# A windowed attention and a gated feed-forward in one kernel: the inverse of the fourth head pair becomes a list item of its own

## The chip, the cores and the metric

The kernel runs on one core of one Trainium2 chip. The metric is the device time of one execution in microseconds. Below, TensorE is PE in the profile's rows (its weight loads are PEld), VectorE is DVE, ScalarE is ACT, GpSimd is POOL and SyncE is SP. All five run their own instruction streams and wait for each other by semaphores.

## The reference

Attention for 4 batches, 8 heads, 768 positions and 64 channels per head, with a mask that keeps the first 8 keys and the last 96 keys before each query, and a bias that falls with distance. Its output, 3072 tokens of 512 channels, goes straight into a feed-forward with a ReLU gate:

```
scores = scale * q @ k.T + bias(head, distance);  masked where neither global nor local
a = exp(scores - max);  a = a / (sum(a) + 1e-9)
x = (a @ v), heads side by side                      # 3072 x 512
out = (relu(x @ w_gate) * (x @ w_val)) @ w_out       # 512 -> 1536 -> 512
```

## The kernel before

**Halves.** The work is cut into eight halves of 384 tokens (a batch has two). For each half c there is attention, which fills the tile xT (the attention output, transposed, 128 x 4 x 384), and the feed-forward, which reads it. Attention of half c+1 is woven into the feed-forward of half c: the halves 2 to 7 are made by `attention_pieces(s)`, and the weaving runs in the feed-forward of half 1 (with the rest of half 0) and of halves 2 to 6. These are the "later halves" of the change. Halves 0 and 1 are written out by hand with other functions, and the feed-forward of half 7 has no attention beside it.

**Feed-forward of a half.** Twelve blocks f = 0 to 11 of hidden channels. For each block a gate product g(f), four matmuls with 384 columns into one PSUM bank (L745), which ACT empties with a ReLU into the tile grelu (L754), and a value product v(f), four more matmuls, which DVE multiplies with the ReLU into ht (L761). Then the output products, seven groups p1, p2, p4, p6, p5, p7, p3 for a pair of token tiles (L631; a Strassen-like scheme whose sums of ht, the tiles hsum, DVE makes at L624 to L627, whose first result ACT copies at L660, and whose other results DVE adds at L644). Odd halves from 3 on have seven more, for a pair of tiles across two halves. So an even half has 24 + 7 = 31 products and an odd half 24 + 14 = 38; the first weave, in halves 0 and 1, has 38 too.

**Attention of a half.** Four pairs of heads p = 0 to 3. The list that `attention_pieces` returns has these items: U0, U1, U2 score two groups each (L512, four PSUM banks, of which the first is from the pool of two "av" banks and three are from the pool of three "qk" banks); X takes one of those banks through the exponential on ACT (L521) and puts the mask multiplication of the one before it on DVE (L533); AVp, two items e = 0 and 1 for the two heads, multiplies the weights with the values (L431, one "av" bank each; half of the 128 rows is the sum of the weights, which the ones beside the values give) and puts the logarithm of that sum on ACT (L440, tile lnd). The second of the two also puts the exponential of minus the logarithm, the inverse, on ACT (L445, tile rcp). Np, the norms, are two DVE multiplications of 64 rows by 384 columns (L450), which write xT, read the "av" banks and so set them free.

**Order.** The kernel writes its own order; every engine takes its instructions in the order in which the code gives them. `weave` walks through the products of the feed-forward, all of equal weight, and after each of them puts out the attention items whose place has been reached. The places come from `spread`, which divides a stretch evenly by the number of items in the list:

```
n = len(items)
return [(first + (i + 0.5) / n * (last - first), f) for i, (_, f) in enumerate(items)]
```

The stretch is 0.02 to 0.86 of the products in the first weave, 0 to 0.87 in even halves and 0 to 0.85 in odd ones. "Place k" below is the place straight after the k-th product of the weave: in even and odd halves g(0) is product 1, v(0) product 2, up to v(11), product 24, and p1 is product 25. The list also holds empty items (`wait`) that only take a share of the stretch.

**Banks.** PSUM has eight banks here: three of the pool "qk", two of "av", three of "ff" (the products of the feed-forward). When a tile is asked for, the pool gives the bank that was set free first, and the first matmul into it waits for whoever read that bank last.

Of the kernel before, what the change touches and what calls it, by code (L numbers as in the profile page):

```python
# [8 lines left out]
FP32 = mybir.dt.float32  # L9
BF16 = mybir.dt.bfloat16  # L10
FP16 = mybir.dt.float16
AF = mybir.ActivationFunctionType
# [4 lines left out]
def kernel(  # L17
# [12 lines left out]
    nc = tc.nc  # L30
# [6 lines left out]
    N_DC = DM // 128  # L37
    N_FC = DFF // 128
    HP = H // 2
    QH = S // 2  # L40
# [6 lines left out]
    scale = 1.0 / math.sqrt(D)  # L47
# [22 lines left out]
    rc_pool = ctx.enter_context(tc.tile_pool(name="rc", bufs=2))  # L70
    xt_pool = ctx.enter_context(tc.tile_pool(name="xt", bufs=3))
# [180 lines left out]
    xT_of = {}  # L252
    es_of = {}
    av_of = {}
# [165 lines left out]
    def piece_av(s, p, e):  # L420
        b, half = divmod(s, 2)
        h = 2 * p + e
        vb = vbuf[b % 2]
        av = av_psum.tile([128, 512], FP32, name="av_ps")
        av_of[s, p, e] = av
        av3 = av[:, 0:QH].rearrange("d (n p) -> d n p", n=NN)
        todo = [t for bank in banks_of_half[half] for t in bank]
        for i, (j, a, w, m) in enumerate(todo):
            es, c = es_of[s, p, j, e]
            z0 = 2 * D * h + (D if e == 0 else 0)  # L430
            nc.tensor.matmul(av3[:, :, a : a + w],  # L431
                             lhsT=vb[:, j, z0 : z0 + 128],
                             rhs=es[:, c : c + NN * w].rearrange("k (n p) -> k n p", n=NN),
                             start=(i == 0), stop=(i == len(todo) - 1),
                             skip_group_check=True)
        o0, d0 = (0, 64) if e == 0 else (64, 0)
        if e == 0:
            av_of[s, p, "l"] = rc_pool.tile([128, QH], FP32, name="lnd")
        ln = av_of[s, p, "l"]
        nc.scalar.activation(ln[o0 : o0 + 64], av[d0 : d0 + 64, 0:QH], AF.Ln, bias=0.0, scale=1.0)  # L440
        if e == 1:
            if s not in xT_of:
                xT_of[s] = xt_pool.tile([128, N_DC, QH], BF16, name="xT")
            rc = rc_pool.tile([128, QH], FP32, name="rcp")
            nc.scalar.activation(rc, ln, AF.Exp, bias=0.0, scale=-1.0)  # L445
            av_of[s, p, "r"] = rc

    def piece_norm(s, p, e):
        r = slice(64 * e, 64 * e + 64)
        nc.vector.tensor_tensor(xT_of[s][r, p, :], av_of[s, p, e][r, 0:QH], av_of[s, p, "r"][r],  # L450
                                op=ALU.mult)

    def piece_av_wide(s, p, *pools):

        b, half = divmod(s, 2)
        todo = [t for bank in banks_of_half[half] for t in bank]
        pools = pools or (AVB,)
        av = [pool.tile([128, 512], FP32, name=name) for pool, name in (pools[0], pools[-1])]
        for what in range(2):
            av3 = av[what][:, 0:QH].rearrange("d (n p) -> d n p", n=NN)  # L460
            for i, (j, a, w, m) in enumerate(todo):
                for e in range(2):
                    es, ce = es_of[s, p, j, e]
                    z0 = D + 2 * D * (2 * p + e)
                    nc.tensor.matmul(av3[64 * e : 64 * e + 64, :, a : a + w],  # L465
                                     lhsT=ones if what == 0 else vbuf[b % 2][:, j, z0 : z0 + D],
                                     rhs=es[:, ce : ce + NN * w].rearrange("k (n p) -> k n p", n=NN),
                                     start=(i == 0), stop=(i == len(todo) - 1),
                                     skip_group_check=True)
        av_of[s, p] = av  # L470

    def piece_norm_wide(s, p):
        piece_sums_wide(s, p)
        piece_mul_wide(s, p)
# [20 lines left out]
    def score_unit(s, groups, pools):  # L495


        b, half = divmod(s, 2)
        out = []
        for pp, g in groups:  # L500
            banks = []
            for e in range(2):
                pool, name = pools.pop(0)
                banks.append(pool.tile([128, 512], FP32, name=name))
                out.append((pp, g, e, banks[e]))
            c = 0
            for j, a, w, m in banks_of_half[half][g]:
                for p in (2 * pp, 2 * pp + 1):
                    for e in range(2):
                        r = slice(64 * e, 64 * e + 64)  # L510
                        q3 = qT2[s % 2][r, p].rearrange("d (n p) -> d n p", n=NN)
                        nc.tensor.matmul(banks[e][:, c : c + NN * w], lhsT=kT[b % 2][p][r, j, :],  # L512
                                         rhs=q3[:, :, a : a + w], start=True, stop=True)
                    c += NN * w
        return out

    def unit_exp(s, pp, g, e, ps):
        bank = banks_of_half[s % 2][g]
        cols = sum(2 * NN * w for _, _, w, _ in bank)
        es = es_pool.tile([128, 480], BF16, name="es")  # L520
        nc.scalar.activation(es[:, 0:cols], ps[:, 0:cols], AF.Exp, bias=0.0, scale=scale)  # L521

        def mask():
            c = 0
            for j, a, w, m in bank:
                n_ = 2 * NN * w
                e4 = es[:, c : c + n_].rearrange("k (i n p) -> k i n p", i=2, n=NN)
                h0 = 4 * pp + e
                mk = m_all[:, h0 : h0 + 3 : 2, 0 if j == 0 else 1, :, m : m + w]
                if w == WQ:  # L530
                    e4 = e4.rearrange("k i n p -> k i (n p)")
                    mk = mk.rearrange("k i n p -> k i (n p)")
                nc.vector.tensor_mul(e4, e4, mk)  # L533
                for i in range(2):
                    es_of[s, 2 * pp + i, j, e] = (es, c + i * NN * w)
                c += n_

        return mask

    def attention_pieces(s):  # L540
        masks, units = [], []

        def flush():
            for f in masks:
                f()
            masks.clear()

        def scores(groups, pools):
            units.extend(score_unit(s, groups, list(pools)))

        def x(scored=None):
            ready = masks[:]
            masks.clear()
            if scored:
                scores(*scored)
            masks.append(unit_exp(s, *units.pop(0)))
            for f in ready:
                f()

        U = [([(0, 0), (0, 1)], (AVB, QKB, QKB, QKB)),  # L560
             ([(0, 2), (1, 0)], (AVB, QKB, QKB, QKB)),
             ([(1, 1), (1, 2)], (AVB, QKB, QKB, QKB))]
        X = lambda u=None: [(0.0, lambda: x(u))]
        AV = lambda p: [(0.0, lambda e=e: (flush(), piece_av(s, p, e))) for e in range(2)]
        N = lambda p: [(0.0, lambda: (piece_norm(s, p, 0), piece_norm(s, p, 1)))]
        wait = [(0.0, lambda: None)]
        a0, a1 = AV(0), AV(1)

        return (X(U[0]) + X() + X() + X() + wait + X(U[1]) + X() + X() + a0[0:1] + X() + a0[1:2] + N(0) + wait
                + X(U[2]) + X() + a1[0:1] + X() + X() + a1[1:2] + N(1) + wait * 2 + AV(2) + N(2) + wait * 2  # L570
                + AV(3) + N(3))


    out_v = out.rearrange("(s p n) d -> s n p d", p=128, n=NN)
# [262 lines left out]
    def AV(s, p, *pools):  # L837
        piece_av_wide(s, p, *pools)
        piece_norm_wide(s, p)
# [139 lines left out]
    def T2_piece(p):  # L979
# [10 lines left out]
    sums_wo = [(0.0, f) for i in (0, 3) for f in weight_sums(i, i + 3)]  # L990
    weave(f1_0[G[2]] + f1_1[G[2]] + f2_0 + f2_1,
          spread(attention_pieces(2), 0.02, 0.86), spread(early_pieces(3), 0.1, 0.76),
          spread(sums_wo, 0.08, 0.4))

    for c in range(2, NHALF):
        placed = []
        if c + 1 < NHALF:
            placed.append(spread(attention_pieces(c + 1), 0.0, 0.85 if c % 2 else 0.87))
        if c + 2 < NHALF:
            load_qk(c + 2, 0, H)  # L1000
            load_v_half(c + 2)
            placed.append(spread(early_pieces(c + 2), 0.25, 0.75))
        f1, f2 = ffn_pieces(c)
        weave(f1 + f2, *placed)
# [35 lines left out]
```

The softmax here doesn't subtract the row's maximum and nothing guards it: scores larger than these inputs give would overflow.

## Time and profile before

| What | Value |
|---|---|
| device time, median of 3 runs | 238.54 us (237.76 to 238.59) |
| profiled execution: span | 236.1 us |
| feed-forward of halves 2 to 7 starts at | 75.78, 100.33, 129.31, 154.04, 183.03, 207.58 us |
| so even halves 2, 4, 6 take | 24.55, 24.73, 24.55 us |
| and odd halves 3, 5 take | 28.98, 28.99 us |
| L440 logarithms | 48, 485 ns each |
| L445 exponentials of logarithms | 24, 523 ns each |
| L450 norms | 48, 553 ns each |
| L761 products of gate and value | 96, 557 ns each |
| L745 matmuls | 768, 155.8 us of PE's 228.7 us busy |

The starts of the halves are read from the timeline of PE, at the first gate product of each. In a timeline line the columns are the start (us), the length (us), the engine, the line of code, the operation with what it writes and reads, and how many instructions are merged; brackets hold idle time of the engine before it and what ended that. In a waits line the three numbers are the sum (us), how often, and the longest (us).

### The profile page before, as it was taken

The page shows a single profiled execution, that of the slowest core. Times are in us where ns is not written, and L with a number is a line of the kernel's source. Part 1 is how long each engine was busy: PE and PEld are TensorE (multiplying, and loading weights), DVE is VectorE, ACT ScalarE, POOL GpSimd, SP SyncE. Part 2 cuts the span into 40 slices and gives each one's busy share as a digit, 9 for nine tenths or more (in the row PEclk, how much of TensorE's full clock was granted, in tenths as well). Part 3 has the DMA queues.
Part 4 walks back from the last instruction along what each step waited for, and adds up shares of the span by engine and source line. Part 5 has one row for each costly group of instructions (what it writes and reads, how often), then busy time and mean ns, then how long its engine had stood idle before and what let it go on. Part 6 is the DMA issues. An engine that isn't in the chain of part 4 may idle for free.

```text
span 236.1 us, 5512 instructions
## 1 busy us (share of the span) xinstructions
PE 228.7 (97%) x2021; PEld 157.7 (67%) x2021; DVE 186.9 (79%) x466; ACT 146.2 (62%) x321; POOL 89.0 (38%) x191
## 2 busy tenths in 40 slices
PE   7898999999999999999999999999999999999994
PEld 3674766656678666856688566856688566865683
DVE  6876867879988779886999779876899779863784
ACT  7988865667624887467842787557742687624310
POOL 8997913933483066406580066405340000000000
PEclk9999999999999999999999999999999999999999
DMA  5999999998459856856397764846412200020005
GB/s 167 203 168 183 206 262 282 171 118 267 72 155 170 250 149 106 52 176 204 90 81 119 236 175 90 53 143 214 93 44 89 92 0 3 0 92 0 1 3 178
DMA packets 71419, 30.43 MB, mean 129 GB/s; under 512 B 47744, under 2 KB 70784, under 8 KB 71392
## 3 DMA queue, kind: packets, MB, share of 16 engines
q0 software_dynamic: 34896, 10.27, 38.7%
q1 hardware_dynamic: 36496, 19.82, 29.7%
q8 instruction: 16, 0.26, 0.5%
q14 instruction: 11, 0.09, 0.1%
HBM read 28.38 MB, written 6.29 MB: 147 GB/s over the span
## 4 chain that ended last, share of the span: by engine, by line
PE 83%; DVE 5%; POOL 4%; DMA 4%; ACT 2%; issue 1%; POOLq 0%; DVEq 0%
PE ff_ps L745 49%; PE ff_ps L631 19%; PE av_ps L431 6%; DMA kc<-in_q_dram 4%; PE ff_ps L778 2%; PE av_ps L512 2%; PE qk_ps L512 2%; POOL vbuf L154 1%; DVE wo_sum L597 1%; DVE obuf L644 1%; DVE ht L761 1%; DVE es L533 1%; POOL kc L131 1%; PE av_ps L465 1%; POOL wg L171 1%
## 5 line engine op out<-in xcount | busy, mean ns | idle before, releaser
L754 ACT ACTIVATE grelu<-ff_ps 128x384 bf16<-128x384 f32 x96 | 46.8, 489 | 52.6 <-PE ff_ps L745 39.3
L745 PE MATMUL ff_ps<-xT,wg 128*128 128x384 bf16 x384 | 77.9, 326 | 0.2 <-DMA wg<-in_moe_w_gate_dram 0.2
L745 PE MATMUL ff_ps<-xT,wv 128*128 128x384 bf16 x384 | 77.9, 326 | 0.0
L761 DVE TENSOR_TENSOR ht<-ff_ps,grelu 128x384 f16<-128x384 f32 x96 | 53.4, 557 | 27.6 <-PE ff_ps L745 23.5
L745 PEld LDWEIGHTS <-wv 128*128 128x128 bf16 x384 | 36.0, 98 | 23.9 <-issue 1.1
L745 PEld LDWEIGHTS <-wg 128*128 128x128 bf16 x384 | 36.3, 97 | 21.7 <-issue 0.7
L450 DVE TENSOR_TENSOR xT<-av_ps,rcp 64x384 bf16<-64x384 f32 x48 | 26.6, 553 | 6.1 <-ACT rcp L445 5.3
L367 POOL CAST kc<-ks 128x384 bf16<-128x384 f32 x20 | 10.6, 569 | 54.5 <-DMA ks<-in_k_dram 54.5
L644 DVE TENSOR_TENSOR obuf<-ff_ps,obuf 128x512 f32<-128x512 f32 (+1 forms) x46 | 27.6, 604 | 3.6 <-PE ff_ps L631 0.9
L440 ACT ACTIVATE lnd<-av_ps 64x384 f32<-64x384 f32 x48 | 23.3, 485 | 11.1 <-PE av_ps L431 10.2
L533 DVE TENSOR_TENSOR es<-es,m_all 128x432 bf16<-128x432 bf16 (+3 forms) x108 | 29.9, 321 | 0.2 <-ACT es L521 0.2
L521 ACT ACTIVATE es<-qk_ps 128x432 bf16<-128x432 f32 (+2 forms) x54 | 27.6, 531 | 0.0
L154 POOL DMA_DIRECT2D vbuf<-in_v_dram x29 | 24.7, 860 | 0.1
L431 PEld LDWEIGHTS <-vbuf 128*128 128x128 bf16 x216 | 18.2, 98 | 4.8 <-DVE xT L450 0.4
L431 PE MATMUL av_ps<-es,vbuf 128*128 128x216 bf16 (+4 forms) x216 | 21.4, 226 | 0.0
L631 PEld LDWEIGHTS <-ht 128*128 128x128 f16 x198 | 18.6, 97 | 3.5 <-issue 0.8
L631 PEld LDWEIGHTS <-hsum 128*128 128x128 f16 x192 | 18.5, 98 | 2.1
L631 PE MATMUL ff_ps<-wo_sb,ht 128*128 128x256 f16 x132 | 18.3, 272 | 0.0
L631 PE MATMUL ff_ps<-wo_sum,hsum 128*128 128x256 f16 x144 | 17.2, 272 | 0.0
L445 ACT ACTIVATE rcp<-lnd 128x384 f32<-128x384 f32 x24 | 12.6, 523 | 0.8
L521 ACT ACTIVATE es<-av_ps 128x432 bf16<-128x432 f32 (+2 forms) x18 | 9.5, 527 | 2.0 <-PE qk_ps L512 2.0
L512 PEld LDWEIGHTS <-kT 64*128 64x128 bf16 x216 | 6.6, 94 | 6.1 <-issue 3.8
(130 smaller groups left out, 263.6 us busy)
## 6 DMA issues: line engine op xcount, KB each, us to landing
out_dram<-obuf SPq DMA_DIRECT2D x22, 256.0 KB
ks<-in_k_dram SPq DMA_DIRECT2D x5, 768.0 KB
qs<-in_q_dram SPq DMA_DIRECT2D x5, 768.0 KB
vbuf<-in_v_dram POOLq DMA_DIRECT2D x23, 120.0 KB, 4.7
wv<-in_moe_w_val_dram POOLq DMA_DIRECT2D x3, 512.0 KB, 10.5
wo_sb<-in_moe_w_out_dram POOLq DMA_DIRECT2D x1, 1536.0 KB, 21.0
wg<-in_moe_w_gate_dram POOLq DMA_DIRECT2D x2, 512.0 KB, 10.3
ks<-in_k_dram SPq DMA_DIRECT2D x4, 192.0 KB
```

The lines of the kernel that those rows point to most:

```text
L154: nc.gpsimd.dma_start(out=v_dst(b, NG + r0, NG + r0 + n, j), in_=v[b, :, KT * j + r0 : KT * j + r0 + n, :].rearrange("h p d -> p h d"))
L431: nc.tensor.matmul(av3[:, :, a : a + w], lhsT=vb[:, j, z0 : z0 + 128], rhs=es[:, c : c + NN * w].rearrange("k (n p) -> k n p", n=NN), star ...
L440: nc.scalar.activation(ln[o0 : o0 + 64], av[d0 : d0 + 64, 0:QH], AF.Ln, bias=0.0, scale=1.0)
L450: nc.vector.tensor_tensor(xT_of[s][r, p, :], av_of[s, p, e][r, 0:QH], av_of[s, p, "r"][r], op=ALU.mult)
L512: nc.tensor.matmul(banks[e][:, c : c + NN * w], lhsT=kT[b % 2][p][r, j, :], rhs=q3[:, :, a : a + w], start=True, stop=True)
L521: nc.scalar.activation(es[:, 0:cols], ps[:, 0:cols], AF.Exp, bias=0.0, scale=scale)
L533: nc.vector.tensor_mul(e4, e4, mk)
L631: nc.tensor.matmul(ps[:, c0 : c0 + DH], lhsT=lhs(i), rhs=rhs(i), start=(i == 0), stop=(i == NP - 1), skip_group_check=True)
L644: add = lambda o, x, y: nc.vector.tensor_tensor(o, x, y, op=ALU.add)
L745: nc.tensor.matmul(st[key][:, 0:QH], lhsT=w_of(w, dc, fc), rhs=xT_of[c][:, dc, :], start=(dc == 0), stop=(dc == N_DC - 1))
L754: nc.scalar.activation(gr, psg[:, 0:QH], AF.Relu, bias=0.0, scale=1.0)
L761: nc.vector.tensor_tensor(ht[:, fc, :], psv[:, 0:QH], st["r", fc], op=ALU.mult)
```

## The change

The exponential of the logarithms of pair 3 is taken out of the item that holds the second half of AV3 and becomes an item of the list by itself, between AV3 and its norms N3. It is meant to let other ACT work pass between logarithm and exponential, and to keep the norms from being queued on DVE before their factor is there. The pairs 0 to 2 keep logarithm and exponential in one item. The tile xT is asked for where the first norm is written, and no longer where the first exponential is; this moves no instruction.

```
-        if e == 1:
-            if s not in xT_of:
-                xT_of[s] = xt_pool.tile([128, N_DC, QH], BF16, name="xT")
-            rc = rc_pool.tile([128, QH], FP32, name="rcp")
-            nc.scalar.activation(rc, ln, AF.Exp, bias=0.0, scale=-1.0)
-            av_of[s, p, "r"] = rc
+        if e == 1 and p < HP - 1:
+            piece_inverse(s, p)
+
+    def piece_inverse(s, p):
+        rc = rc_pool.tile([128, QH], FP32, name="rcp")
+        nc.scalar.activation(rc, av_of[s, p, "l"], AF.Exp, bias=0.0, scale=-1.0)
+        av_of[s, p, "r"] = rc
 
     def piece_norm(s, p, e):
+        if s not in xT_of:
+            xT_of[s] = xt_pool.tile([128, N_DC, QH], BF16, name="xT")
...
         return (X(U[0]) + X() + X() + X() + wait + X(U[1]) + X() + X() + a0[0:1] + X() + a0[1:2] + N(0) + wait
                 + X(U[2]) + X() + a1[0:1] + X() + X() + a1[1:2] + N(1) + wait * 2 + AV(2) + N(2) + wait * 2
-                + AV(3) + N(3))
+                + AV(3) + [(0.0, lambda: piece_inverse(s, 3))] + N(3))
```

The list has 30 items before and 31 after.

## The prediction

> **What bounds the kernel now.** I read the page first: engine shares, the granted clock and the chain that ended last.
>
> ```profile
> PE 228.7 (97%) x2021; PEld 157.7 (67%) x2021; DVE 186.9 (79%) x466; ACT 146.2 (62%) x321; POOL 89.0 (38%) x191
> ...
> PEclk9999999999999999999999999999999999999999
> ...
> PE 83%; DVE 5%; POOL 4%; DMA 4%; ACT 2%; issue 1%; POOLq 0%; DVEq 0%
> ```
>
> TensorE is busy 97% of the span at full clock and carries 83% of the chain, so a wait put into its stream lengthens the kernel by its full length. The timeline says whether "busy" is also full speed: in an even half a product of four 384-column matmuls starts every 0.65 us (84.85 to 85.50 below), 162 ns a matmul, and the same from product to product. Waits that TensorE could still lose are few. The waits views of the weight loads and of VectorE, in that order, show where it is near to waiting:
>
> ```profile
> PEld L512 <- DVE xT L450: 2.1, 6, 0.5
> ...
> PEld L431 <- DVE xT L450: 0.4, 1, 0.4
> ```
>
> ```profile
> DVE xT L450 <- ACT rcp L445: 5.3, 14, 0.9
> ```
>
> The scores of L512 and the value products of L431 take over an "av" bank from a norm at L450, and most of these six L512 lines stand for norms that end just as TensorE arrives. The norms in turn wait for the inverse, 14 times of 24. So the chain that matters is value product, logarithm, inverse, norm, next user of the bank. The timelines of an even half (c = 2) for PE, ACT and DVE, from 84 to 99 us, give its margins:
>
> ```profile
> 84.85 0.81 PE L745 MATMUL ff_ps<-xT,wv 128*128 128x384 bf16 x4
> 85.50 0.81 PE L745 MATMUL ff_ps<-xT,wg 128*128 128x384 bf16 x4
> 86.25 0.25 PE L512 MATMUL av_ps<-qT,kT 64*128 64x192 bf16 x1
> ...
> 89.67 0.47 PE L431 MATMUL av_ps<-es,vbuf 128*128 128x72 bf16 x5
> ...
> 92.58 0.47 PE L431 MATMUL av_ps<-es,vbuf 128*128 128x72 bf16 x5
> ```
>
> ```profile
> 90.39 0.48 ACT L440 ACTIVATE lnd<-av_ps 64x384 f32<-64x384 f32 x1
> 90.90 0.52 ACT L445 ACTIVATE rcp<-lnd 128x384 f32<-128x384 f32 x1
> ```
>
> ```profile
> 85.50 1.14 DVE L450 TENSOR_TENSOR xT<-av_ps,rcp 64x384 bf16<-64x384 f32 x2
> ...
> 90.90 0.56 DVE L761 TENSOR_TENSOR ht<-ff_ps,grelu 128x384 f16<-128x384 f32 x1
> 91.37 0.41 DVE L625 TENSOR_TENSOR hsum<-hsum,ht 128x512 f16<-128x512 f16 x1
> 91.70 1.13 DVE L450 TENSOR_TENSOR xT<-av_ps,rcp 64x384 bf16<-64x384 f32 x2
> 92.87 0.56 DVE L761 TENSOR_TENSOR ht<-ff_ps,grelu 128x384 f16<-128x384 f32 x1
> ```
>
> The scores U2 start at 86.25; the norm whose bank they take (the first of the two from 85.50) ends at 85.50 + 1.14/2 = 86.07, only 0.18 us earlier. The second half of AV1 starts at 89.67, its inverse is ready at 90.90 + 0.52 = 91.42, its norms N1 begin at 91.70 behind the product of v(8) and a sum, and AV2, which takes their bank, starts at 92.58. All margins are a fraction of one 0.65 us place.
>
> **What the Trainium skill says.** "Perfetto Trace Analysis", Identifying the Most-Contended Engine: matmul busy share is no measure of the peak; this trace agrees in that the 97% alone proves nothing, and the 162 ns spacing does. "TensorE: Matmul & The Clock Gate", Back-to-back issue gap, prices an isolated warm matmul at N/2.4 + 2.5 ns, 162.5 ns for 384 columns; the trace has 162. The same page, Architectural detail: VectorE and ScalarE are strict first-in-first-out, and of TensorE's stream only weight loads are pulled ahead. The trace agrees: no VectorE product passes a norm that waits for its inverse. "Perfetto Trace Analysis", Optimization Strategy: equal bubbles on the saturated engine can mean too few PSUM buffers, which is the two-bank "av" pool here.
>
> **The change, part by part.** No instruction is added or removed; the exponential, its length and count stay.
>
> *The split itself.* In every later half the exponential stays where it was (place 26 in even halves) and so do the norms N3 (27). Cost nothing: N3 waits for an inverse queued one product earlier, and p4, p6, p5, p7 and p3 run before the next half reads it.
>
> *The longer list.* `spread` divides by 31 in place of 30, so every item sits earlier: item i moves from (i + 0.5)/30 to (i + 0.5)/31 of the stretch. Counted out, in even halves U2 moves from place 13 to 12, its second X from 14 to 13, N1 from 18 to 17, AV2 from 21 and 22 to 20 and 21, N2 from 23 to 22, AV3 from 25 and 26 to 24 and 25. N0 stays at 11, AV1 at 14 and 17. So U2 comes one product after N0 instead of two, and N1 is queued with its own logarithm, before the product of v(8) rather than after it. The built order shows the same on VectorE in all three even halves. In odd halves X, AV0 and N0 move together and U2 stays, and AV2, N2 and AV3 move together; in the first weave all from U2 to AV3 move together.
>
> *Even halves, U2.* TensorE ends v(5) at 85.50 and, with the 0.10 us that the switch to the 64-row matmuls takes in this trace (86.25 - 85.50 - 0.65), asks for the bank at 85.60. N0's first norm still ends at 86.07. From there to the matmul I take 0.05 us (in the first weave a norm ended at 59.28 and U2 started at 59.33). Wait: 86.12 - 85.60 = 0.52. The same sum at c = 4 (norm from 139.02, v(5) ends 139.03) and c = 6 (192.74, 192.75) gives 0.51 each. Sum 1.54 us.
>
> *Even halves, AV2 on N1.* Count from the start of AV1's second half. The inverse ends at 1.75 (91.42 - 89.67), N1 starts at 1.79, its first norm is done at 2.36, AV2 may start at 2.41. TensorE asks at 2.91 - 0.65 = 2.26, because one product fewer lies between. Wait 0.15. At c = 4 such a wait of 0.18 exists already (asked 146.10, started 146.28) and is replaced, not added.
>
> *Even halves, what queues behind N1 on VectorE.* While VectorE holds N1 for its inverse, the product of v(8) stands behind it though its inputs are there; then come the sum of L625, v(9), L626, v(10), L627 and N2. With the starts' spacing in the trace (norms 1.17, products 0.47, sums 0.33, 0.46 and 0.47) N1 starts at 1.79, v(8) at 2.96, v(9) at 3.76, v(10) at 4.69, N2 at 5.64, and its first norm lets go at 6.26. TensorE: AV2 2.41 to 2.71, g(10) to 3.36, AV2 to 3.66, v(10) to 4.31. g(11) takes the bank of v(9), free at 3.76 + 0.56 + 0.05 = 4.37: wait 0.06. g(11) and v(11) run to 5.67, where AV3 now stands, one product earlier; it needs N2's bank, at 6.26: wait 0.59. Before, AV3 asked after p1 (95.79), with N2's first norm done at 95.68, no wait. After AV3 nothing is short: the DVE work up to N3 is as before and TensorE arrives later.
>
> Per even half 0.52 + 0.15 + 0.06 + 0.59 = 1.32, three times 3.96, less the 0.18: **+3.78 us**.
>
> *Odd halves.* The copy of L660 for the second seven products stands on ScalarE behind the logarithm and inverse of pair 3, and p4 waits for it:
>
> ```profile
> 125.20 0.52 ACT L445 ACTIVATE rcp<-lnd 128x384 f32<-128x384 f32 x1
> ...
> 125.63 0.35 ACT L660 COPY obuf<-ff_ps 128x256 f32<-128x256 f32 x1
> ...
> 126.04 0.82 PE L631 MATMUL ff_ps<-wo_sum,ht 128*128 128x256 f16 x6
> ```
>
> p4 asked at 125.81 and lost 0.23. With AV3 one product earlier both are done sooner and the copy is free to start when p1 ends. AV2's first half now also stands between v(11) and p1, which before lost 0.09 (118.74 to 118.83) on the ReLU of g(11). Two odd halves with attention beside them (3 and 5): **-0.64 us**. N0 there comes nearly one product earlier against an unmoved U2, a margin on a wait of zero.
>
> *First weave.* U2 asks one product sooner, but N0 no longer stands behind a 0.7 us weight sum on VectorE; U2 followed by v(11) ends where v(11) followed by U2 ended. Zero.
>
> Sum: +3.78 - 0.64 = +3.14, so 238.54 + 3.14 = 241.7.
>
> **Unknown costs.** What the trace does not have is a wait of this kind in the middle of an even half. Lower bound: only the two waits whose both sides the trace shows directly, U2 (0.52) and AV2 (0.15). Upper bound: the VectorE row as slow as at c = 4, where GpSimd is busy beside it and L533 took 1.01 where it takes 0.67, and L625 0.60 where it takes 0.41: 0.5 us more per half before AV3. I take the spacing of c = 2, which c = 6 repeats.
>
> **Rivals.**
> 1. *Forecast*, 241.7: all four waits.
> 2. *VectorE catches up*: the idle time that U2's wait gives it lets it clear its row, and AV3 doesn't wait. 3 x 0.67 - 0.18 - 0.64 = +1.2, 239.7. For it: 0.46 us of idle VectorE at 87.23. Against: that idle time lies before N1, and what delays the row is the inverse, which moves with TensorE.
> 3. *Not slower*: the split does what it is for, the even halves' waits are hidden behind earlier value products, and only the odd gain and the 0.18 are left: -0.82, 237.7. For it: 5.3 us of VectorE waiting for the inverse. Against: only pair 3 is split, and U2's 0.52 needs no assumption but the place.
> 4. *Deeper*: the upper bound in all three halves and no odd gain, 3.78 + 1.5 = +5.3, 243.8. For it: late products on VectorE can also hold back g(10) or v(10). Against: after the change these take banks of g(9)'s ReLU and v(8), both free in time by the sum above.
>
> **How the numbers follow.** Forecast 0.60, rival 2 0.20, rival 3 0.06, rival 4 0.14. The time is the forecast's. The range leaves out rival 3 and the far half of rivals 2 and 4: 239.4 to 243.0. Half a per cent is 1.2 us: the forecast and rival 4 are slower by more, and half of rival 2; the other half and most of rival 3 are within it; a remainder is faster. Slower 0.84, same 0.13, faster 0.03.
>
> **What would show it.** U2 in even halves preceded by about 0.5 us of idle TensorE ended by L450; in the waits of PEld, L512 and L431 on L450 rising from 2.5 us to over 5; VectorE idle before N1 on the inverse where it had none at 91.70; AV3 of even halves waiting about 0.6 us for N2; between first gate products the even halves at 25.9 us (24.55, 24.73, 24.55 before) and the odd ones at 28.7 (28.98, 28.99). I am wrong if the even halves keep their length, if a wait sits on another bank (grelu or ht before L745), or if halves 3 and 5 grow.

## The result, and the profile after

The changed kernel takes 241.09 us, median of six runs (240.05 to 241.32), against 237.95 us for the kernel before in its six runs (236.97 to 238.59). That is 3.14 us more, a ratio of 1.013 with a 95% interval of 1.009 to 1.016. In the profiled executions the span goes from 236.1 to 239.5 us. Line numbers over about 440 are three higher in the changed kernel: the inverse is now L446, the norms L453, the scores L515, the gate and value matmuls L748.

The same parts of the page as before, engine shares, granted clock and chain:

```profile
PE 230.0 (96%) x2021; PEld 157.7 (66%) x2021; DVE 189.1 (79%) x466; ACT 147.5 (62%) x321; POOL 89.2 (37%) x191
...
PEclk9999999999999999999999999999999999999999
...
PE 77%; POOL 7%; DVE 5%; DMA 5%; ACT 3%; issue 1%; POOLq 0%; DVEq 0%
```

The instruction counts and the clock are unchanged and TensorE is busy only 1.3 us longer (230.0 against 228.7), so most of the 3.4 us of span is TensorE standing still. The waits of the weight loads say for whom:

```profile
PEld L515 <- DVE xT L453: 3.5, 6, 0.8
PEld L431 <- DVE xT L453: 2.7, 6, 0.5
```

These two sums were 2.1 and 0.4 us; now they are 6.2 together. The value products of L431 waited once and now wait six times, twice in each even half. The number of waits of L515 is still six, but longer.

The stretches between the first gate products of the halves place the loss:

| Half | 2 | 3 | 4 | 5 | 6 |
|---|---|---|---|---|---|
| before, us | 24.55 | 28.98 | 24.73 | 28.99 | 24.55 |
| after, us | 25.86 | 28.66 | 25.87 | 28.71 | 25.59 |
| difference, us | +1.31 | -0.32 | +1.14 | -0.28 | +1.04 |

Together +3.49 in even halves and -0.60 in odd ones, 2.9 of the 3.4 us. The other 0.5 us lies ahead of half 2: its start was at 75.78 and is at 76.28 us. Over the profiled runs of all kernels below this start scatters from 74.9 to 76.4 us, and `late_order` and `no_order`, which have the same first weave, start at 75.46 and 75.37. The first weave itself did not lose it: from its first gate product to the first one of half 2 it took 28.87 us before and takes 28.74 after. The lag is there when it begins, at 46.91 us before and at 47.53 after, in code that the change does not touch.

Now the even half c = 2 of the changed kernel, the timeline of PE (the L515 matmuls after the first are left out):

```profile
85.35 0.81 PE L748 MATMUL ff_ps<-xT,wv 128*128 128x384 bf16 x4
86.60 0.25 PE L515 MATMUL av_ps<-qT,kT 64*128 64x192 bf16 x1 [0.43 <-DVE xT L453]
...
92.27 0.81 PE L748 MATMUL ff_ps<-xT,wv 128*128 128x384 bf16 x4
93.06 0.48 PE L431 MATMUL av_ps<-es,vbuf 128*128 128x72 bf16 x5
...
94.34 0.81 PE L748 MATMUL ff_ps<-xT,wv 128*128 128x384 bf16 x4
95.33 0.81 PE L748 MATMUL ff_ps<-xT,wg 128*128 128x384 bf16 x4 [0.18 <-DVE ht L764]
95.98 0.81 PE L748 MATMUL ff_ps<-xT,wv 128*128 128x384 bf16 x4
96.93 0.48 PE L431 MATMUL av_ps<-es,vbuf 128*128 128x72 bf16 x5
```

The end of a product is taken as its start plus 0.65 us, the spacing of products that follow without a wait; what comes after that, and after the 0.10 us of the switch to 64-row matmuls for the scores, is lost. There are four such gaps, at the four places of the prediction. U2 asks at 85.35 + 0.65 + 0.10 = 86.10 and starts at 86.60: 0.50 us. AV2 asks at 92.92 and starts at 93.06: 0.14. g(11) asks at 94.99 and starts at 95.33: 0.34. AV3 asks at 96.63 and starts at 96.93: 0.30. They make 1.28 of the 1.31 us. AV2 and AV3 carry no bracket in these rows, since a merged row of 0.81 us reaches 0.16 past the next start; the rows of their weight loads carry 0.36 and 0.53, which is more than TensorE lost. The size of a loss is read from start to start.

What held them is in the timelines of ACT and DVE for the same stretch:

```profile
91.39 0.48 ACT L440 ACTIVATE lnd<-av_ps 64x384 f32<-64x384 f32 x1
91.90 0.52 ACT L446 ACTIVATE rcp<-lnd 128x384 f32<-128x384 f32 x1
```

```profile
85.99 1.14 DVE L453 TENSOR_TENSOR xT<-av_ps,rcp 64x384 bf16<-64x384 f32 x2
...
92.46 1.14 DVE L453 TENSOR_TENSOR xT<-av_ps,rcp 64x384 bf16<-64x384 f32 x2 [0.23 <-ACT rcp L446]
93.63 0.56 DVE L764 TENSOR_TENSOR ht<-ff_ps,grelu 128x384 f16<-128x384 f32 x1
94.10 0.71 DVE L628 TENSOR_TENSOR hsum<-hsum,ht 128x512 f16<-128x512 f16 x1
94.73 0.55 DVE L764 TENSOR_TENSOR ht<-ff_ps,grelu 128x384 f16<-128x384 f32 x1
...
96.33 1.14 DVE L453 TENSOR_TENSOR xT<-av_ps,rcp 64x384 bf16<-64x384 f32 x2
```

N0's first norm ends at 85.99 + 0.57 = 86.56 and U2 starts 0.04 later. N1 waits 0.23 us for its inverse (ready 91.90 + 0.52 = 92.42) with the product of v(8) behind it, and its first norm ends at 93.03, 0.03 before AV2. The product of v(9) ends at 94.73 + 0.55 = 95.28, 0.05 before g(11). N2's first norm ends at 96.90, 0.03 before AV3. The one row that isn't as in the working is the sum at 94.10: 0.71 us, where before it was 0.41.

In the odd half c = 3, p4 waits for the copy of L663. Two timelines of PE, before and after, show the row of p1 and p2 ahead of p4 (`x12`, two products):

```profile
124.51 1.47 PE L631 MATMUL ff_ps<-wo_sb,ht 128*128 128x256 f16 x12
126.04 0.82 PE L631 MATMUL ff_ps<-wo_sum,ht 128*128 128x256 f16 x6
```

```profile
126.22 1.47 PE L634 MATMUL ff_ps<-wo_sb,ht 128*128 128x256 f16 x12
127.53 0.82 PE L634 MATMUL ff_ps<-wo_sum,ht 128*128 128x256 f16 x6
```

and the timeline of ACT after shows the copy:

```profile
126.27 0.52 ACT L446 ACTIVATE rcp<-lnd 128x384 f32<-128x384 f32 x1
127.07 0.37 ACT L663 COPY obuf<-ff_ps 128x256 f32<-128x256 f32 x1 [0.28 <-PE ff_ps L634]
```

The inverse ends at 126.79, ScalarE is idle for 0.28 us and the copy now starts when p1 lets it (before, it stood directly behind the inverse). p4 starts 1.31 us after p1, which is two products of 0.65 without a gap; before, it was 1.53.

### The profile page after: what moved, and what is told of

It is laid out like the page before. It is cut to its first block, busy times and chain, and to the rows that moved or that the text cites. A ratio compares the mean times of both kernels' runs of the same rounds, so it can differ in the third digit from the quotient of the medians.

```text
span 239.5 us, 5510 instructions
## 1 busy us (share of the span) xinstructions
PE 230.0 (96%) x2021; PEld 157.7 (66%) x2021; DVE 189.1 (79%) x466; ACT 147.5 (62%) x321; POOL 89.2 (37%) x191
## 4 chain that ended last, share of the span: by engine, by line
PE 77%; POOL 7%; DVE 5%; DMA 5%; ACT 3%; issue 1%; POOLq 0%; DVEq 0%
PE ff_ps L748 45%; PE ff_ps L634 20%; PE av_ps L431 5%; DMA wv<-in_moe_w_val_dram 5%; POOL vbuf L154 3%; PE av_ps L515 2%; PE ff_ps L781 2%; PE qk_ps L515 2%; DVE ht L764 1%; DVE xT L453 1%; POOL kc L131 1%; DVE obuf L647 1%; POOL wg L171 1%; ACT lnd L440 1%; ACT grelu L757 1%
## 5 line engine op out<-in xcount | busy, mean ns | idle before, releaser
L748 PE MATMUL ff_ps<-xT,wg 128*128 128x384 bf16 x384 | 77.9, 326 | 1.3 <-DMA wg<-in_moe_w_gate_dram 0.9
L748 PE MATMUL ff_ps<-xT,wv 128*128 128x384 bf16 x384 | 77.9, 326 | 0.3 <-DMA wv<-in_moe_w_val_dram 0.3
L764 DVE TENSOR_TENSOR ht<-ff_ps,grelu 128x384 f16<-128x384 f32 x96 | 53.3, 556 | 29.8 <-PE ff_ps L748 24.8
L748 PEld LDWEIGHTS <-wg 128*128 128x128 bf16 x384 | 36.4, 97 | 23.9 <-issue 2.0
L748 PEld LDWEIGHTS <-wv 128*128 128x128 bf16 x384 | 35.9, 98 | 23.3 <-DMA wv<-in_moe_w_val_dram 0.6
L536 DVE TENSOR_TENSOR es<-es,m_all 128x432 bf16<-128x432 bf16 (+3 forms) x108 | 32.2, 340 | 0.2 <-ACT es L524 0.2
L453 DVE TENSOR_TENSOR xT<-av_ps,rcp 64x384 bf16<-64x384 f32 x48 | 26.6, 554 | 5.2 <-ACT rcp L446 4.2
L431 PEld LDWEIGHTS <-vbuf 128*128 128x128 bf16 x216 | 17.8, 98 | 7.4 <-DVE xT L453 2.7
L431 PE MATMUL av_ps<-es,vbuf 128*128 128x216 bf16 (+4 forms) x216 | 21.5, 226 | 0.4 <-DVE xT L453 0.2
L634 PE MATMUL ff_ps<-wo_sum,hsum 128*128 128x256 f16 x144 | 17.7, 272 | 0.0
L446 ACT ACTIVATE rcp<-lnd 128x384 f32<-128x384 f32 x24 | 12.6, 523 | 0.7
L515 PEld LDWEIGHTS <-kT 64*128 64x128 bf16 x216 | 6.6, 94 | 7.5 <-issue 3.8
```

Source lines behind the costliest of these rows:

```text
L431: nc.tensor.matmul(av3[:, :, a : a + w], lhsT=vb[:, j, z0 : z0 + 128], rhs=es[:, c : c + NN * w].rearrange("k (n p) -> k n p", n=NN), star ...
L634: nc.tensor.matmul(ps[:, c0 : c0 + DH], lhsT=lhs(i), rhs=rhs(i), start=(i == 0), stop=(i == NP - 1), skip_group_check=True)
L748: nc.tensor.matmul(st[key][:, 0:QH], lhsT=w_of(w, dc, fc), rhs=xT_of[c][:, dc, :], start=(dc == 0), stop=(dc == N_DC - 1))
L764: nc.vector.tensor_tensor(ht[:, fc, :], psv[:, 0:QH], st["r", fc], op=ALU.mult)
```

## The experiments

The theory: the separate inverse costs nothing, and the whole effect comes from the list being one item longer, through four waits per even half and one removed per odd half. The rivals: the inverse's own place costs time; or one of the four waits brings the others, so that without it the half would be cured. Placement is edited with a variant of `spread`, in which chosen items take their place from a list of 31 and all others keep their place of the list of 30:

```
+    def spread_as(items, first, last, long=(), own=28, extra=None):
+        out = []
+        for i, (_, f) in enumerate(items):
+            x = (i + 0.5) / 31 if i in long else ({29: own, 30: 29}.get(i, i) + 0.5) / 30
+            x += (extra or {}).get(i, 0.0)
+            out.append((first + x * (last - first), f))
+        return out
```

`own` is the place of the inverse: 28 is with the second half of AV3, as before, and 29 with N3. Items 12 to 14 are an empty one, U2 and its X; 19 is N1; 22 and 23 are AV2, 24 is N2, 27 and 28 are AV3. Each group of runs had the kernel before on the same chip: 237.72 us (`empty`, `split`, `even`, `odd`), 237.70 us (`u2`, `n1`, `tail`, `best`), 237.46 us (`late_order`) and 237.60 us (`no_order`, `odd_first`). Here are the lengths of the halves in all of them:

| us | 2 | 3 | 4 | 5 | 6 |
|---|---|---|---|---|---|
| `empty` | 25.59 | 28.66 | 25.72 | 28.67 | 25.58 |
| `split` | 24.55 | 28.80 | 24.74 | 28.75 | 24.55 |
| `even` | 25.59 | 28.98 | 25.58 | 29.24 | 25.58 |
| `odd` | 24.55 | 28.66 | 24.55 | 28.67 | 24.55 |
| `u2` | 25.10 | 28.98 | 25.05 | 28.98 | 25.05 |
| `n1` | 24.91 | 29.02 | 24.91 | 29.36 | 24.91 |
| `tail` | 25.33 | 28.97 | 25.66 | 28.98 | 25.33 |
| `best` | 24.67 | 28.67 | 24.67 | 28.67 | 24.67 |
| `late_order` | 25.60 | 28.67 | 25.86 | 28.66 | 25.59 |
| `no_order` | 25.67 | 28.66 | 25.59 | 28.83 | 25.59 |
| `odd_first` | 24.55 | 28.67 | 24.55 | 28.67 | 24.55 |

### The longer list alone: `empty`

The kernel before with one more empty item; the inverse stays in AV3's item.

```
-                + AV(3) + N(3))
+                + AV(3) + wait + N(3))
```

> Kernel before, with an empty item put into the list between AV3 and N3, so that the list has 31 items; the inverse of pair 3 stays in AV3's own item. Theory (the longer list moves the places, and that is the whole cost): about 3.1 us over the kernel before, as with the change; even halves 25.6 to 25.9 us between first gate products, odd ones 28.7. Rival (the separate exponential costs the time): as the kernel before, within 0.5 us.

Measured: 239.93 us, +2.21, ratio 1.010 (1.007 to 1.014). The waits of the weight loads:

```profile
PEld L512 <- DVE xT L450: 3.5, 6, 0.8
PEld L431 <- DVE xT L450: 2.7, 6, 0.5
```

These are the sums of the changed kernel to the tenth, without the change's code: one item that does nothing, in a list whose length divides the stretch, is enough for the waits on norms. The odd halves have their gain as well. About 3.1 us were expected; the interval (1.7 to 3.3 us) does not exclude that, but the even halves are 0.27 (c = 2) and 0.15 us (c = 4) shorter than in the changed kernel, nearly all of it in the wait of g(11), 0.09 and 0.22 us here. That the separate inverse makes this rest is ruled out below: `even` has the changed kernel's code and places in its even halves and the same short waits.

### The separate inverse alone: `split`

The changed code, with the old places for every other item and the inverse one place later, with N3.

```
-          spread(attention_pieces(2), 0.02, 0.86), ...
+          spread_as(attention_pieces(2), 0.02, 0.86, own=29), ...
-            placed.append(spread(attention_pieces(c + 1), 0.0, 0.85 if c % 2 else 0.87))
+            placed.append(spread_as(attention_pieces(c + 1), 0.0, 0.85, own=29) if c % 2 else
+                          spread_as(attention_pieces(c + 1), 0.0, 0.87, own=29))
```

> The inverse of pair 3 as an item of its own, one place later than before (with N3, behind one more product), while every other item keeps the place it had in the list of 30. Theory: no time is lost; the even halves stay at 24.55 to 24.73 us, and the odd ones gain up to 0.23 us each because the copy of L663 now stands ahead of that exponential on ScalarE: 0 to 0.5 us under the kernel before. Rival (the separate exponential costs the time): 3 us over it.

Measured: 237.08 us, -0.64, ratio 0.997 (0.996 to 0.998). The sum of L515 on L453 is 1.9 us in six waits, and L431 has its one of 0.4, as before. Even halves are as before; the odd ones are 0.18 and 0.24 us shorter, so 0.4 of the 0.64 us is placed, and the interval (0.4 to 0.9) leaves the rest open. The timeline of c = 3 shows what the change was meant to do, and does where the inverse really comes one place later:

```profile
123.63 1.47 PE L634 MATMUL ff_ps<-wo_sb,ht 128*128 128x256 f16 x12
...
124.48 0.37 ACT L663 COPY obuf<-ff_ps 128x256 f32<-128x256 f32 x1 [0.19 <-PE ff_ps L634]
...
124.75 0.53 ACT L446 ACTIVATE rcp<-lnd 128x384 f32<-128x384 f32 x1
124.94 0.82 PE L634 MATMUL ff_ps<-wo_sum,ht 128*128 128x256 f16 x6
```

The copy goes ahead of the inverse, and p4 starts with no gap, where before it lost 0.23 us.

### The longer list in even or in odd halves only: `even` and `odd`

```
# even
+            placed.append(spread_as(attention_pieces(c + 1), 0.0, 0.85) if c % 2 else
+                          spread_as(attention_pieces(c + 1), 0.0, 0.87, long=range(31)))
# odd
+            placed.append(spread_as(attention_pieces(c + 1), 0.0, 0.85, long=range(31)) if c % 2 else
+                          spread_as(attention_pieces(c + 1), 0.0, 0.87))
```

In both, the first weave has the old places. Lines that remove the old call are left out here and below.

> The places of the 31-item list in the even halves only; first weave and odd halves keep the places of before. Theory: even halves 1.31, 1.14 and 1.04 us longer as in the changed kernel, odd ones unchanged: 3.5 us over the kernel before. Rival (all woven parts share the cost evenly): 1.9 us.

> The places of the 31-item list in the odd halves only; first weave and even halves keep the places of before. Theory: odd halves 0.3 us shorter each, the even ones unchanged: 0.6 us under the kernel before. Rival (what the odd halves gain is only waiting moved from the even ones): no change, within 0.2 us.

Measured: `even` 241.26 us, +3.54, ratio 1.016 (1.013 to 1.019); `odd` 236.93 us, -0.79, ratio 0.997 (0.996 to 0.998). So the loss is in the even halves and the odd places are a gain, -0.32 us in each of halves 3 and 5. The even halves of `even` grew by 1.04, 0.85 and 1.03 us, less than the 1.31, 1.14 and 1.04 expected, since g(11) waits 0.09, 0.06 and 0.06 us there; the total agrees because c = 5 lost 0.26 us that the working doesn't have: its p2 waits 0.25 us for a product of L764. In `odd` the wait of 0.18 us that the kernel before has in c = 4 is gone too. The timelines of DVE show its row unslowed there: the mask multiplications ahead of N1 take 0.67 us instead of 1.01 and the sum 0.42 instead of 0.60, with GpSimd's copies of keys about 0.3 us later against the start of the half.

### Each step of the even halves by itself: `u2`, `n1`, `tail`

All others at the old places, only these items of the even halves one product earlier:

```
# u2:   long=(12, 13, 14)        U2 and its second X
# n1:   long=(19,)               N1
# tail: long=range(20, 30)       AV2, N2, AV3
```

> Places of before, only U2 and its second exponential one product earlier in the even halves. Theory: TensorE waits 0.50 us for N0's first norm in each of the three and nothing else changes: 1.5 us over the kernel before. Rival (a wait there is made up later, where TensorE waits for VectorE anyway): under 0.5 us.

> Places of before, only N1 one product earlier in the even halves, so that VectorE holds it for its inverse with the product of v(8) queued behind it; AV2, N2 and AV3 stay. Theory: by itself this costs TensorE little, at most 0.2 us per half at g(11), as AV2 and AV3 still ask late: 0 to 0.6 us over the kernel before. Rival (a blocked VectorE queue is the main cost of the change): 1.5 us or more.

> Places of before, only AV2, N2 and AV3 one product earlier in the even halves; U2 and N1 stay. Theory: AV2 then waits 0.4 us for N1 behind the product of v(8) and a sum, AV3 0.3 us for N2: 1.9 us over the kernel before. Rival (AV2 and AV3 wait only because N1 was put in front): under 0.5 us.

`u2`: 238.91 us, +1.21, ratio 1.005 (1.004 to 1.007). U2 waits 0.50 us in each even half, and those grow by 0.55, 0.32 and 0.50, 1.37 in sum against 1.5 expected: in c = 4 the old wait of 0.18 us goes as TensorE comes later.

`n1`: 239.16 us, +1.46, ratio 1.006 (1.004 to 1.008), where 0 to 0.6 was expected: a miss. The even halves grow by 0.36, 0.18 and 0.36. The timelines of PE and DVE in c = 2:

```profile
92.83 0.47 PE L431 MATMUL av_ps<-es,vbuf 128*128 128x72 bf16 x5
93.41 0.81 PE L748 MATMUL ff_ps<-xT,wv 128*128 128x384 bf16 x4
```

```profile
91.62 1.14 DVE L453 TENSOR_TENSOR xT<-av_ps,rcp 64x384 bf16<-64x384 f32 x2 [0.56 <-ACT rcp L446]
92.80 0.56 DVE L764 TENSOR_TENSOR ht<-ff_ps,grelu 128x384 f16<-128x384 f32 x1
```

The five matmuls of AV2 take 0.31 us from start to start and here 0.58: v(10) waits 0.27 us for the bank of v(8), whose product stands behind the waiting N1 and ends at 93.36. Just before, g(10) waits 0.09 us and starts 0.05 after the ReLU of g(9), which stands behind the inverse on ScalarE. So N1 ahead of that product has a price of its own, which the changed kernel hides: there AV2, which then stands ahead of g(10), waits instead. In c = 5, whose places are those of before, the same wait of p2 as in `even` comes back, 0.37 us, so that about 0.9 of the 1.46 us lie in the even halves. Copies of GpSimd run beside it; that they cause it is not shown.

`tail`: 240.63 us, +2.93, ratio 1.013 (1.010 to 1.015), where 1.9 was expected; by the lengths of the halves it is 2.5. The timeline of PE in c = 2:

```profile
91.75 0.48 PE L431 MATMUL av_ps<-es,vbuf 128*128 128x72 bf16 x5 [0.21 <-DVE xT L453]
...
95.35 0.48 PE L431 MATMUL av_ps<-es,vbuf 128*128 128x72 bf16 x5 [0.21 <-DVE xT L453]
```

AV2 waits 0.38 us (0.71 in c = 4, where the mask multiplications ahead of N1 take 1.04 us instead of 0.67 beside copies of GpSimd) and AV3 0.38. With N1 at its old place, behind the product and the sum, AV2 loses more than the 0.14 of the changed kernel. The three pieces cost 0.50 + 0.36 + 0.78 = 1.64 us in c = 6 apart and 1.04 together. They are not additive: N1 moved ahead shortens AV2's wait from 0.38 to 0.14, and each wait delays TensorE for the ones after it. U2 waits without the other moves, and AV2 and AV3 wait without those of U2 and N1, so no single wait brings the rest.

### A try at keeping only the gain: `best`

Odd halves with the places of 31, the first weave with the inverse at N3, and in even halves the first item of AV2 one product later, against the 0.18 us of c = 4.

```
+            placed.append(spread_as(attention_pieces(c + 1), 0.0, 0.85, long=range(31)) if c % 2 else
+                          spread_as(attention_pieces(c + 1), 0.0, 0.87, extra={22: 0.03}))
```

> The places of the 31-item list in the odd halves, those of before in the even halves with the first item of AV2 one product later, and in the first weave the inverse of pair 3 with N3. Theory: 0.8 us under the kernel before, no wait of TensorE over 0.12 us in halves 2 to 6. Rival (the gains of the odd halves are lost elsewhere): within 0.3 us of the kernel before.

Measured: 237.31 us, -0.39, ratio 0.998 (0.997 to 1.000), half of what was expected. AV3 now loses 0.125 us in every even half, c = 2 and c = 6 too, which had nothing to gain: moving AV2 was a mistake.

### What stretches the sum in front of v(9)'s product: `late_order`, `no_order`

In the changed kernel the sum L628 takes 0.71 us in c = 2 and c = 4 and 0.41 in c = 6, and g(11) waits 0.35, 0.35 and 0.06 us. In c = 6 GpSimd has no half left to prepare; in the others it copies keys at that time. Its timeline in c = 2:

```profile
93.68 0.20 POOL L279 COPY kT<-kN 128x24 bf16<-128x24 bf16 x1
...
94.00 0.53 POOL L278 COPY kT<-kN 128x360 bf16<-128x360 bf16 x1
94.48 0.40 POOL L279 COPY kT<-kN 128x24 bf16<-128x24 bf16 x1
```

The sum runs from 94.10 to 94.81, and the small copy beside it takes twice the time of the one at 93.68. `late_order` moves these copies to a later place in the list; `no_order` leaves them out in halves 2 and 4, so that the attention of halves 4 and 6 reads older keys.

```
# late_order
+            early = spread(early_pieces(c + 2), 0.25, 0.75)
+            if c % 2 == 0:
+                early = early[:-HP] + spread([(0.0, f) for _, f in early[-HP:]], 0.74, 0.82)
+            placed.append(early)
# no_order
+            early = spread(early_pieces(c + 2), 0.25, 0.75)
+            placed.append(early if c % 2 else early[:-HP])
```

> The changed kernel, with the last four of GpSimd's early items (the copies of keys into kT for the half after next) moved behind the place where N1 and what follows it stand on VectorE, in even halves. Theory (TensorE's wait at g(11) of halves 2 and 4 is made by GpSimd's copies, which stretch L536 and L628 on VectorE): that wait falls from 0.35 to 0.06 us or less in both halves, as it is in half 6, where GpSimd is idle; halves 2 and 4 take 25.6 instead of 25.9 us. Rival (the wait is made by the order on VectorE alone): 0.35 us stays.

> The changed kernel without GpSimd's copies of keys into kT that run in halves 2 and 4 (their attention is then computed with older keys). Theory (these copies lengthen the sum of L628 on VectorE, and g(11) waits for what comes behind it): L628 takes 0.42 us in all three even halves and g(11) loses 0.06 us, as in half 6; the even halves take 25.6 us each, 0.5 us less in sum than in the profile of the changed kernel. Rival (the order on VectorE alone): g(11) still loses 0.3 us or more in halves 2 and 4.

`late_order`: 240.58 us, +3.12, ratio 1.013 (1.010 to 1.016), but the run settles nothing. The first copy of c = 2 waited 3.06 us for a transfer (kN<-kc), so that a later place in the list did not move the copies on the chip as planned; in c = 2 the sum took 0.45 us, in c = 4 still 0.70.

`no_order`: 240.12 us, +2.52, ratio 1.012 (1.009 to 1.016). The timeline of DVE in c = 2:

```profile
92.80 0.56 DVE L764 TENSOR_TENSOR ht<-ff_ps,grelu 128x384 f16<-128x384 f32 x1
93.28 0.41 DVE L628 TENSOR_TENSOR hsum<-hsum,ht 128x512 f16<-128x512 f16 x1
93.61 0.55 DVE L764 TENSOR_TENSOR ht<-ff_ps,grelu 128x384 f16<-128x384 f32 x1
```

With no copies the sum takes 0.41 us in all three even halves, and g(11) waits 0.06 in each, as predicted. Two other waits are longer than in the changed kernel, U2 in c = 2 by 0.08 us and p2 in c = 5 by 0.12. Here are the sum's length and g(11)'s wait wherever they differ, over four kernels:

| L628 (L625 in `empty`), us | 0.415 | 0.446 | 0.575 | 0.703 | 0.714 |
|---|---|---|---|---|---|
| wait of g(11), us | 0.06 | 0.089 | 0.219 | 0.347 | 0.357 |

The wait is the sum's length less 0.36 us, everywhere. The Trainium skill, "SBUF — State Buffer", in the section on the two separate sides, has VectorE and GpSimd arbitrate for a shared port pair when the VectorE operation has two SBUF inputs and the GpSimd one reads SBUF. The sum has two inputs in SBUF; the products beside the same copies have one in PSUM and keep their 0.55 us. The page calls the pair an exclusive lock; what the changed kernel shows of it is 0.29 us more on a sum of 0.41. In c = 4 of `odd` it is the other way round: the sum starts 0.01 us ahead of a copy of 56 columns and keeps its 0.42 us, and the copy takes 0.49 instead of 0.22. How much g(11) waits thus depends on where the copies fall in that run.

### A version that beats both: `odd_first`

The even halves as before, odd halves with the places of 31, the first weave with the inverse at N3.

```
+          spread_as(attention_pieces(2), 0.02, 0.86, own=29), ...
+            placed.append(spread_as(attention_pieces(c + 1), 0.0, 0.85, long=range(31)) if c % 2 else
+                          spread_as(attention_pieces(c + 1), 0.0, 0.87))
```

> The places of the 31-item list in the odd halves, those of before in the even halves, and in the first weave the inverse of pair 3 with N3, one place later. Theory: the 0.6 us of the odd halves and the 0.18 us of half 4, nothing from the first weave, where TensorE has no wait for the attention: 0.8 us under the kernel before. Rival (the lower start of half 2 in the profile of the kernel with only the split was a gain of the first weave): 1.5 us or more under it.

Measured: 236.77 us, -0.83, ratio 0.997 (0.996 to 0.998). By lengths it is -0.18 (c = 4), -0.31 and -0.32, the same as `odd` (-0.79): the inverse's place in the first weave adds nothing that can be seen.

## Why the prediction was right

The forecast added 3.14 us to the time before, and 3.14 was measured, with an interval of 2.2 to 3.8; the kernel before ran 0.59 us below its earlier median in that comparison, hence 241.09 against 241.7. The mechanism held: all four waits stand where the working had them, and the separate inverse is not their cause. Step by step for the even halves:

| Step | predicted, each | measured, c = 2, 4, 6 | sum predicted | sum measured |
|---|---|---|---|---|
| U2 on N0 | 0.52, 0.51, 0.51 | 0.50, 0.50, 0.50 | 1.54 | 1.50 |
| AV2 on N1 | 0.15 | 0.14, 0.14, 0.14 | 0.45 | 0.42 |
| g(11) on v(9)'s product | 0.06 | 0.35, 0.35, 0.06 | 0.18 | 0.76 |
| AV3 on N2 | 0.59 | 0.30, 0.30, 0.32 | 1.77 | 0.93 |
| old wait in c = 4 | -0.18 | -0.18 | -0.18 | -0.18 |

The sum was to be 3.78 and is 3.43; the lengths of the halves give 3.49. In the profiled run halves and first weave together lost 2.8 us (3.49 - 0.60 - 0.13), not 3.14. The exact agreement is therefore luck: two terms were mis-sized in opposite directions, and the interval of 2.2 to 3.8 us cannot tell 2.8 from 3.14.

- **AV3.** In the working for what queues behind N1, the spacings 0.46 and 0.47 for the sums now L629 and L630 came from a trace in which VectorE was not backlogged: one holds a wait for the next product, the other a sum slowed from 0.41 to 0.47. The timeline of DVE in c = 6 after shows the backlogged row:

```profile
203.54 0.55 DVE L764 TENSOR_TENSOR ht<-ff_ps,grelu 128x384 f16<-128x384 f32 x1
204.01 0.41 DVE L629 TENSOR_TENSOR hsum<-ht 128x512 f16<-128x512 f16 x1
204.36 0.56 DVE L764 TENSOR_TENSOR ht<-ff_ps,grelu 128x384 f16<-128x384 f32 x1
204.84 0.41 DVE L630 TENSOR_TENSOR hsum<-ht,hsum 128x512 f16<-128x512 f16 x1
205.17 1.13 DVE L453 TENSOR_TENSOR xT<-av_ps,rcp 64x384 bf16<-64x384 f32 x2
```

  They are 0.35 and 0.33, together 0.25 less, and 0.59 - 0.25 = 0.34 is close to what c = 6 lost there (0.32). The 0.33 of the first sum, which the working used two terms earlier, was the right figure for all three.
- **g(11).** The sum of L628 was priced at its undisturbed spacing. The section on unknown costs had seen a sum of 0.60 us beside busy GpSimd and put it into the upper bound only. `no_order` shows that the copies make the difference. In c = 2 and c = 4 AV3 does not wait longer for it: the 0.29 us delay N2 and TensorE alike. With the same code and places in its even halves, `even` waited 0.09, 0.06 and 0.06 us there.

U2, AV2 and the replaced wait held to 0.02 us. The odd halves were to give -0.32 each and gave -0.32 and -0.28, with the copy no longer behind the inverse, as the working had it; in c = 3 p4's gap gave 0.22 of it and p1's 0.09. For the first weave I said zero, and its length went from 28.87 to 28.74 us: U2 waited 0.22 us for N0 there and now waits 0.09. The four profiles with the list of 31 all have 28.74; with the places of 30 it is 28.87 in five and 28.65 in four, so the term lies between -0.13 and +0.09. What decides between the two lengths stays open. "The split itself costs nothing" was right in `split`, but in the change the inverse keeps its old place only because the longer list moves it back: put one place later, it gains 0.2 us per odd half, which the working did not look for.

Rival 2 (VectorE catches up) falls by AV3's 0.3 us in every even half; rival 3 (not slower) by the even lengths; rival 4 (deeper) by the odd gain and by AV3's wait being shorter than forecast, not longer. The waits sum of 6.2 us (over 5 was asked for), the lengths of the halves (25.9 in c = 2 and 4, 28.7 in the odd ones) and VectorE's idle 0.23 us ahead of N1 came as listed; c = 6 took 25.6, and AV3 waited 0.3 us where about 0.6 was listed.

## What to carry to other kernels

Where items are placed by dividing a stretch by their number, adding an item moves every other one; count out which of them pass a product, and look at the margins there, before looking at the item itself. A queue's delay is worked out with the lengths that its rows have when backlogged, not with the spacings of a trace in which they waited, and with what other engines do to them at that time. Try the added item and the moved places apart: here the places of even halves lost 3.5 us, and those of odd halves alone gained 0.8.

## What the runs showed of the hardware

A VectorE sum with both inputs in SBUF (128 x 512, f16) takes 0.41 us, and up to 0.71 us with key copies of GpSimd beside it; the copy of 24 columns goes from 0.20 to 0.40 us at the same moment. Two mask multiplications of 128 x 432, also with both inputs in SBUF, take 0.67 us and up to 1.04 beside such copies. Products with one input in PSUM stay at 0.55 to 0.56. From the end of a norm or product on VectorE to the matmul that waited for its bank, it is 0.03 to 0.05 us.
